# Causal masks and maxima in a routed attention kernel: who adds, who subtracts, who copies

## The chip, the cores and the metric

The program runs on one core of one Trainium2 chip. The metric is the device time of one execution in microseconds (us); a version is compared by the median of its runs. Engines are named as in the profile: PE (TensorE matmul, with PEld for its weight loads), DVE (VectorE), ACT (ScalarE), POOL (GpSimd), SP (SyncE, which here only issues transfers). PSUM is the memory that PE writes its results to, in banks of 512 fp32 columns; SBUF is the working memory.

## The reference

Sparse attention over 8 batches, 8 heads, 576 positions, 64 dimensions, then a mixture of experts over the 4608 tokens that it yields. Everything is fp32.

```python
scores = q @ k.T / 8
mask_local   = (rel >= 0) & (rel < 32)                              # heads 0-3, rel = row - column
mask_strided = (rel >= 0) & (column % 32 == row % 32)               # heads 4-7
scores = where(mask, scores, -1e9); scores -= max(scores)
x = softmax(scores) @ v                                             # (4608, 512)
do_compute = x @ w_skip > 0;  e = argmax(x @ w_gate)
out = x;  out[do_compute] += gate * relu(x @ w1[e]) @ w2[e]         # one of 8 experts per token
```

## The kernel before

**Units.** Attention is cut into 32 units, four to a batch (`UNITS`, line 33): local heads in blocks of 64 queries by 96 keys, blocks 0 to 3 (unit 0) and 4 to 8 (unit 1), and strided heads as 11 blocks of 54 by 54, blocks 0 to 5 (unit 2) and 6 to 10 (unit 3). A unit (b, u) is unit u of batch b. It passes through these functions:

- `qk` (line 186): on PE the scores of the unit (line 196, four 64x64 corners of the array in turn, fp32) into the PSUM tile S. S spans two banks and there is **one** of it. On DVE the mask is added on the way from S to the SBUF tile `sm` (lines 203, 205, 210: tables of 0 and -2^33), which frees S; then DVE takes the row maxima of `sm` (line 216), and POOL subtracts them in two halves (line 219), in place for local units, into the padded tile `frame` for strided ones.
- `tex` (line 224): PE transposes of the result into PSUM tiles T (line 239), ACT exponentials out of them (line 247).
- `pv` (line 252): PE matmuls with the values into the single PSUM tile PV (lines 269, 282), DVE divides by the row sums (lines 290 to 296) and frees PV.
- `xpose` (line 312): PE transposes (lines 327, 337) and ACT copies of the attention output; `score` (line 358): PE matmuls of a batch with the router weights (line 362), ACT copies (lines 366, 367).

**Routing.** `route1` turns the router scores of a group of batches (PE, line 382), copies them with ACT (line 384) and picks the expert on DVE in nine small instructions (lines 390 to 408), with a few small POOL ones (lines 413 to 417). `route2` counts ranks on PE (lines 426 to 433), gets slots on DVE (438 to 443) and POOL scatters the tokens into a table (line 456). `shift` (line 180) copies the values by 32 rows for odd blocks, in two ACT copies a batch (line 183). `wdma` fetches an eighth of an expert's weights into one of three buffers `raw`; `wsplit` (line 566) splits it into a high part (ACT, line 572) and a rest (DVE, line 573).

**Order.** A loop over the 32 units writes the program of PE, DVE and POOL in the order of the code (`manual_schedule`); ACT's order is chosen by a scheduler. Turn n does: `qk` of unit n+2 on PE; `tex` of unit n; `pv` of unit n-1; then, on DVE, the mask of unit n+2, the division of unit n-1, and the maxima of unit n+2; then `xpose` of unit n-2, the router scores of the last batch (turn of a unit 2), and the pieces of routing and of weight splitting that are due. I call "turn (b, u)" the turn whose `tex` is unit (b, u). Every engine works its own list strictly in order. After the loop the experts' matmuls (lines 631 to 633, 670, 674) run on PE until the end.

Of the kernel before, what the change touches and what calls it, by code (L numbers as in the profile page):

```python
# [23 lines left out]
HP = 64  # L24
LW = HP + ST
LB = S // HP
LV = 5
SQ = 3 * NA
SB = 11
SP = 6  # L30
UNITS = [(0, 0, 4), (0, 4, LB), (1, 0, 6), (1, 6, SB)]
# [8 lines left out]
COUNTED = {4: 3, 7: 5}  # L40
PB = 3
CB = 5
SPLITS = [(6, 0), (6, 1), (7, 0), (7, 2)]
FETCH = [(6, 0), (6, 1), (6, 3), (7, 0)]
CE = (96, 3)

# [51 lines left out]
def attn_moe(ctx: ExitStack, tc: tile.TileContext, q, k, vl, vh, vs, w9d, w1d, w2d, cst, out, NB=B):  # L98
    nc = tc.nc
    V, A, G, T = nc.vector, nc.scalar, nc.gpsimd, nc.tensor  # L100
# [9 lines left out]
    ident = con["id"]  # L110
    w9 = constp.tile([128, 4, 64], F32, name="w9")
    tri = constp.tile([128, 128], BF16, name="tri")
    oneb = constp.tile([128, 128], BF16, name="oneb")
    ebb = constp.tile([128, NE], BF16, name="ebb")
    runs = [constp.tile([128, NE], BF16, name=f"run{i}") for i in range(2)]
# [4 lines left out]
    def ps(tag, n=1):  # L120
        return psum.tile([128, n, 512] if n > 1 else [128, 512], F32, name=tag, tag=tag, bufs=bufs[tag])
# [14 lines left out]
        G.memset(fill[:, :, 1:2], 65536)  # L136
        return fill

    sms = [ap.tile([128, 2, (z - a) * (LW, SQ)[kind]], F32, name=f"sm{i}") for i, (kind, a, z) in enumerate(UNITS)]
    frame = [ap.tile([128, 2, 6, HP], F32, name=f"frame{i}") for i in range(2)]  # L140

    qt_, kt_, vt_ = {}, {}, {}
# [37 lines left out]
    def shift(b, k):  # L180
        r0, r1, d, c = SHIFTS[k]
        src, dst = vt_[b, 0][r0:r1, c:c + LV - 1], v2[b % 2][d:d + r1 - r0]
        A.copy(dst.rearrange("p u h c -> p (u h c)"), src.rearrange("p u h c -> p (u h c)"))


    def qk(b, pr):
        kind, b0, b1 = UNITS[pr]
        qt, kt = qt_[b, kind], kt_[b, kind]
        nq, win = ((HP, LW), (SQ, SQ))[kind]
        n = (b1 - b0) * win  # L190
        s = ps("S", 2)
        for blk in range(b0, b1):
            for j in range(2):
                for i in range(2):
                    p = slice(HP * i, HP * i + HP)
                    T.matmul(s[HP * (i ^ j):HP * (i ^ j) + HP, j, (blk - b0) * win:(blk - b0 + 1) * win],  # L196
                             lhsT=qt[p, j, blk * nq:blk * nq + HP], rhs=kt[p, j, blk * nq:blk * nq + win],
                             start=True, stop=True)
        yield
        sm = sms[pr]  # L200
        if kind == 0:
            if b0 == 0:
                V.tensor_tensor(sm, s[:, :, 0:n], con["ml"].unsqueeze(1).broadcast_to([128, 2, n]), op=ALU.add)
            else:
                V.tensor_tensor(sm.rearrange("p j (n w) -> p j n w", w=win),
                                s[:, :, 0:n].rearrange("p j (n w) -> p j n w", w=win),
                                con["ml"][:, LW:2 * LW].unsqueeze(1).unsqueeze(1).broadcast_to([128, 2, b1 - b0, LW]),
                                op=ALU.add)
        else:
            V.tensor_tensor(sm.rearrange("p j (n w) -> p j n w", w=win),  # L210
                            s[:, :, 0:n].rearrange("p j (n w) -> p j n w", w=win),
                            con["ms"].unsqueeze(1).unsqueeze(1).broadcast_to([128, 2, b1 - b0, win]), op=ALU.add)
        yield
        mx = ap.tile([128, 2, b1 - b0], F32, name="mx", tag="mx", bufs=4)
        sw = sm.rearrange("p j (n w) -> p j n w", w=win)
        V.tensor_reduce(mx, sw, axis=AX.X, op=ALU.max)
        e = sw if kind == 0 else frame[pr - 2][:, :, 0:b1 - b0, 0:win]
        for j in range(2):
            G.tensor_tensor(e[:, j], sw[:, j], mx[:, j].unsqueeze(2).broadcast_to([128, b1 - b0, win]), op=ALU.subtract)  # L219
        e_[b, pr] = e  # L220

    e_, pt_ = {}, {}
# [340 lines left out]
                tc.add_manual_dep(i, x.name, SYNC, reason="the tokens come first")  # L563
            raw_[key, j] = raw

    def wsplit(key, j0, j1):
        for j in range(j0, j1):
            raw = raw_.pop((key, j))
            pl, tg, nb = (early, "w1", 4) if j < 4 else (pool["h"], "w2", 2) if j < 6 else (pool["b"], "w2", 4)
            hi = pl.tile([128, 1024], F32R, name=tg + "h", tag=tg + "h", bufs=nb)  # L570
            lo = pl.tile([128, 1024], F32R, name=tg + "l", tag=tg + "l", bufs=nb)
            A.copy(hi, raw)  # L572
            V.tensor_tensor(lo, raw, hi.bitcast(F32), op=ALU.subtract)  # L573
            wt[key, j] = (hi, lo)

    def wload(key, e, j0, j1):
        for j in range(j0, j1):
# [207 lines left out]
    p = ps("T")  # L785
# [3 lines left out]
    def run(*gs):  # L789
        weave(gs, [])  # L790
# [17 lines left out]
    loadq(1, 0)  # L808
    loadk(1, 0)
    loadv(0, 1)  # L810
    for i in range(2):
        G.memset(frame[i], 0.0)
    V.memset(pvp, 0.0)
# [6 lines left out]
    for n, (b, pr) in enumerate(units):  # L820

        if pr % 2 == 0:
            if b + 1 < NB:
                loadv(b + 1, pr // 2)
            if n == 4:
                nc.sync.dma_start(table.rearrange("(p a n) c -> p a (n c)", p=128, a=5),
                                  fill.rearrange("p n c -> p (n c)").unsqueeze(1).broadcast_to(
                                      [128, 5, NE * ESTR // 160]))
        else:
            if n > 4:  # L830
                store(units[n - 4][0], units[n - 4][1] // 2)
# [12 lines left out]
        seq = [tex(b, pr)]  # L844
        if g and pr == 2:
            seq = [xpose(*units[n - 2])] + seq
        for x in front[:-1]:
            next(x)

        if len(front) > 1:  # L850
            run(seq.pop(0))
        next(front[-1])
        rank = []
        if ranked is not None:
            rank = [route2(ranked, of=COUNTED.get(b - 1))]
            for _ in range(tiles(ranked) + 1):
                next(rank[0])
            ranked = None

        if b > CB:  # L860
            run(*late)
            late = []
        for x in front:
            next(x, 0)
        run(*rank, *late, *front)
        late = []
        if b > 0 and pr == 2:
            seq = [score(b - 1, 0), score(b - 1, 1)] + seq
        if n > 1 and not (g and pr == 2):
            seq.append(xpose(*units[n - 2]))  # L870
        run(*seq)
        if g and pr == 2:
            late = [route1(g[0])]
            next(late[0])
        if g and pr == 3:
            if b > CB:
                run(route2(g[0], of=COUNTED.get(b)))
            else:
                ranked = g[0]
        if b == PB + 2 and pr == 0:  # L880
            pick(PB)
        if (b, pr) in SPLITS:
            j = SPLITS.index((b, pr))
            wsplit("e", j, j + 1)
        if b == CB + 2 and pr == 3:
            count(CB)
        if n == 0 or pr == 3 and b + 1 < NB:
            for m in range(2):
                shift(b + (n > 0), m)
        if n == 1:  # L890
            for g in range(len(GROUPS)):
# [12 lines left out]
        if b == CB + 2:  # L904
            if pr == 0:
                assert not sc_
            if pr == 1:
                rows("e", s0, *CE, eng=G)
                gather("e", "e", "e", last=(CB + 1) * S)
# [3 lines left out]
        scat(*sc_.pop(0))  # L913
    with tc.manual_schedule(engines={T.engine, A.engine, V.engine}):
        run(pv(*units[-1]), xpose(*units[-2]), xturn("e"), xpose(*units[-1]))
    store(NB - 1, 0)
    store(NB - 1, 1)
    wdma("e", e0, 5, 7, st_["e"]["taken"])
# [173 lines left out]
```

## Time and profile before

| | us |
|---|---|
| time, median of 3 runs | 452.54 (452.0 to 456.13) |
| the profiled execution: its own time | 450.83 |
| its span, first to last instruction | 449.1 |
| PE busy in the span | 414.5 (92%) |
| DVE / ACT / POOL busy | 257.5 / 203.7 / 162.9 |
| end of the attention loop on PE, about | 178 |
| waits of PE between 84 and 180 us, in the table of stretches | 17.1 |

How to read it: one execution, times from the start of its span. A group row gives a line, an engine, output<-input, the count, busy time, mean ns of one, and after the second bar the idle time just before with what ended it. A row of the timeline gives start, duration, engine, line, and in brackets the idle time before it. "PEclk" is the share of full clock that PE was granted. "issue" is idle time that the trace gives no cause for.

### The profile page before, as it was taken

How to read it: one execution, taken by the hardware profiler on the slowest of the kernel's cores; microseconds unless marked ns; L12 is line 12 of the kernel's file. 1: busy time of each engine (PE TensorE's matmuls, PEld its weight loads, DVE VectorE, ACT ScalarE, POOL GpSimd, SP SyncE). 2: the span in 40 equal slices, each digit the busy share in tenths (PEclk: the TensorE clock that was granted, in tenths of full speed). 3: DMA queues.
4: the chain of work that ended last, by engine and by line, in shares of the span. 5: the costliest groups of instructions: out<-in, count | busy, mean ns of one | idle time of the engine just before them, and what ended most of it. 6: DMA issues, size and time to landing. Idle time of an engine off the chain costs nothing.

```text
span 449.1 us, 12164 instructions
## 1 busy us (share of the span) xinstructions
PE 414.5 (92%) x4959; PEld 375.0 (83%) x4960; DVE 257.5 (57%) x522; ACT 203.7 (45%) x382; POOL 162.9 (36%) x205
## 2 busy tenths in 40 slices
PE   5979979998786877999999999999999999999994
PEld 3868868777665656889899799999999999999984
DVE  4576766658675675362476465464474564755611
ACT  1556555564544635451633343444444534544400
POOL 3443426563848485364023417014023023200201
PEclk8899998999996998899999999999999999999998
DMA  8999996988896323533558477446566466754201
GB/s 288 368 382 324 340 314 168 300 254 303 251 332 133 74 56 107 148 61 85 180 161 224 141 223 219 135 161 208 163 200 186 157 204 193 213 157 158 73 21 42
DMA packets 48600, 86.51 MB, mean 193 GB/s; under 512 B 9271, under 2 KB 25783, under 8 KB 48541
## 3 DMA queue, kind: packets, MB, share of 16 engines
q1 hardware_dynamic: 40861, 75.28, 53.1%
q0 software_dynamic: 7680, 10.42, 8.5%
q8 instruction: 40, 0.66, 0.6%
q14 instruction: 19, 0.16, 0.1%
HBM read 70.64 MB, written 15.63 MB: 192 GB/s over the span
## 4 chain that ended last, share of the span: by engine, by line
PE 69%; DMA 9%; DVE 6%; issue 6%; POOL 3%; SPq 3%; ACT 2%; POOLq 0%; DVEq 0%; ACTq 0%
PE S L631 15%; PE S L633 15%; PE S L632 15%; PE S L196 4%; PE T L239 4%; PE PV L269 3%; DMA out_dram<-x 3%; PE T L362 2%; DMA xg<-out_dram,tab 2%; PE T L625 2%; PE PV L723 2%; PE PV L282 2%; DVE x L296 1%; PE T L337 1%; POOL table L456 1%
## 5 line engine op out<-in xcount | busy, mean ns | idle before, releaser
L711 POOL DMA_INDIRECT out_dram<-ot,tab x25 | 28.0, 1121 | 152.5 <-DVE ot L709 136.5
L631 PE MATMUL S<-xh,w1h 128*128 128x342 f32 (+6 forms) x248 | 78.4, 316 | 0.2 <-DVE hl L644 0.2
L633 PE MATMUL S<-xh,w1l 128*128 128x342 f32 (+6 forms) x248 | 76.7, 309 | 0.0
L632 PE MATMUL S<-xl,w1h 128*128 128x342 f32 (+6 forms) x248 | 76.6, 309 | 0.0
L631 PE MATMUL S<-hh,w2h 128*128 128x288 f32 (+5 forms) x192 | 59.4, 310 | 0.0
L633 PE MATMUL S<-hh,w2l 128*128 128x288 f32 (+5 forms) x192 | 58.1, 303 | 0.0
L632 PE MATMUL S<-hl,w2h 128*128 128x288 f32 (+5 forms) x192 | 57.9, 302 | 0.0
L643 ACT ACTIVATE hh<-S 128x342 fp32r<-128x342 f32 (+6 forms) x64 | 27.9, 437 | 65.6 <-PE S L633 57.9
L573 DVE TENSOR_TENSOR w1l<-raw,w1h 128x1024 fp32r<-128x1024 f32 x32 | 39.0, 1224 | 22.2 <-ACT w1h L572 21.7
L631 PEld LDWEIGHTS S<-xh,w1h 128*128 128x128 f32 x248 | 46.9, 189 | 1.2 <-issue 0.6
L573 DVE TENSOR_TENSOR w2l<-raw,w2h 128x1024 fp32r<-128x1024 f32 x32 | 39.0, 1223 | 14.0 <-ACT w2h L572 9.2
L632 PEld LDWEIGHTS S<-xl,w1h 128*128 128x128 f32 x248 | 46.8, 189 | 0.1
L633 PEld LDWEIGHTS S<-xh,w1l 128*128 128x128 f32 x248 | 46.7, 188 | 0.0
L196 PE MATMUL S<-kt,qt 64*64 64x54 f32 (+1 forms) x1280 | 32.8, 245 | 13.4 <-DVE sm L210 8.2
L644 DVE SCALAR_TENSOR_TENSOR hl<-S,hh 128x342 fp32r<-128x342 f32 (+6 forms) x64 | 30.9, 484 | 24.1 <-ACT hh L643 22.7
L603 POOL DMA_INDIRECT xg<-out_dram,tab x25 | 31.9, 1275 | 33.2 <-issue 10.6
L456 POOL DMA_INDIRECT table<-pay,rdi x38 | 39.8, 1047 | 10.7 <-issue 8.3
L196 PEld LDWEIGHTS S<-kt,qt 64*64 64x64 f32 x1280 | 27.2, 143 | 19.1 <-DVE sm L210 9.3
L219 POOL TENSOR_TENSOR sm<-sm,mx 128x384 f32<-128x384 f32 (+1 forms) x32 | 28.4, 908 | 32.0 <-PE T L239 11.7
L633 PEld LDWEIGHTS S<-hh,w2l 128*128 128x128 f32 x192 | 36.2, 189 | 0.2 <-DVE w2l L573 0.2
L632 PEld LDWEIGHTS S<-hl,w2h 128*128 128x128 f32 x192 | 36.3, 189 | 0.0
L631 PEld LDWEIGHTS S<-hh,w2h 128*128 128x128 f32 x192 | 36.2, 188 | 0.1
(167 smaller groups left out, 845.9 us busy)
## 6 DMA issues: line engine op xcount, KB each, us to landing
raw<-in_w_dram SPq DMA_DIRECT2D x64, 512.0 KB
vt<-in_vs_dram SPq DMA_DIRECT2D x16, 390.0 KB
qt<-in_qp_dram SPq DMA_DIRECT2D x16, 304.0 KB
kt<-in_kp_dram SPq DMA_DIRECT2D x16, 297.0 KB
kt<-in_kp_dram SPq DMA_DIRECT2D x14, 304.0 KB
vt<-in_vl_dram SPq DMA_DIRECT2D x16, 260.0 KB
out_dram<-x SPq DMA_DIRECT2D x8, 512.0 KB
qt<-in_qp_dram SPq DMA_DIRECT2D x14, 288.0 KB
```

Of the source, the lines that this page charges most:

```text
L196: T.matmul(s[HP * (i ^ j):HP * (i ^ j) + HP, j, (blk - b0) * win:(blk - b0 + 1) * win], lhsT=qt[p, j, blk * nq:blk * nq + HP], rhs=kt[p, j ...
L219: G.tensor_tensor(e[:, j], sw[:, j], mx[:, j].unsqueeze(2).broadcast_to([128, b1 - b0, win]), op=ALU.subtract)
L239: T.transpose(t[:w, x * 128:(x + 1) * 128], a, ident)
L456: i = G.indirect_dma_start(out=table, out_offset=bass.IndirectOffsetOnAxis(ap=di[:, t:t + 1], axis=0), in_=pay[:, t, :], in_offset=None, b ...
L573: V.tensor_tensor(lo, raw, hi.bitcast(F32), op=ALU.subtract)
L603: i = G.indirect_dma_start(out=xg[:s["P"], t, :], out_offset=None, in_=out[0:last, :], in_offset=bass.IndirectOffsetOnAxis(ap=s["tab"][:s[ ...
L631: T.matmul(p, lhsT=a[0], rhs=b[0], start=start, stop=False)
L632: T.matmul(p, lhsT=a[0], rhs=b[1], start=False, stop=False)
L633: T.matmul(p, lhsT=a[1], rhs=b[0], start=False, stop=stop)
L643: A.activation(s["hh"][:, f, :C], p[:, :C], AF.Relu)
L644: V.scalar_tensor_tensor(s["hl"][:, f, :C], p[:, :C], 0.0, s["hh"][:, f, :C].bitcast(F32), op0=ALU.max, op1=ALU.subtract)
L711: i = G.indirect_dma_start(out=out, in_=ot[:P], in_offset=None, bounds_check=NTOK - 1, oob_is_err=False, out_offset=bass.IndirectOffsetOnA ...
```

## The change

- PE writes the mask into S first, from bf16 copies of the tables (`mlb`, `msb`) times a bf16 identity (`idb`), four matmuls a unit, and the scores accumulate onto it. The copies are made by DVE at the start.
- DVE takes the maxima straight from S and then subtracts them straight from S; POOL's subtraction is gone, and so are the additions. S is free after the subtraction.
- The value copies of `shift` move from ACT to POOL.
- PE's turning of the router scores moves from the end of one turn to the next turn, behind its `tex`.
- `wsplit` inside the loop is cut in two: ACT's part stays in turns (6, 0), (6, 1), (7, 0), DVE's part comes a turn later, and the fourth piece (turn (7, 2) before) is done after the loop.

```diff
-SPLITS = [(6, 0), (6, 1), (7, 0), (7, 2)]
+CASTS = [(6, 0), (6, 1), (7, 0)]
+RESTS = [(6, 1), (6, 2), (7, 1)]
...
+    mlb = constp.tile([128, 4 * LW], BF16, name="mlb")
+    msb = constp.tile([128, SQ], BF16, name="msb")
+    idb = constp.tile([128, HP], BF16, name="idb")
...
-        A.copy(dst.rearrange("p u h c -> p (u h c)"), src.rearrange("p u h c -> p (u h c)"))
+        G.tensor_copy(dst.rearrange("p u h c -> p (u h c)"), src.rearrange("p u h c -> p (u h c)"))
...
         s = ps("S", 2)
+        hide = mlb if b0 == kind == 0 else (mlb[:, LW:2 * LW], msb)[kind].unsqueeze(1).broadcast_to([128, b1 - b0, win])
+        for j in range(2):
+            for i in range(2):
+                p, g = slice(HP * i, HP * i + HP), slice(HP * (i ^ j), HP * (i ^ j) + HP)
+                T.matmul(s[g, j, 0:n], lhsT=idb[p], rhs=hide[p], start=True, stop=False)
         for blk in range(b0, b1):
...
-                             start=True, stop=True)
-        yield
-        sm = sms[pr]
-        if kind == 0:
-            if b0 == 0:
-                V.tensor_tensor(sm, s[:, :, 0:n], con["ml"].unsqueeze(1).broadcast_to([128, 2, n]), op=ALU.add)
...
+                             start=False, stop=blk == b1 - 1)
         yield
         mx = ap.tile([128, 2, b1 - b0], F32, name="mx", tag="mx", bufs=4)
-        sw = sm.rearrange("p j (n w) -> p j n w", w=win)
+        sw = s[:, :, 0:n].rearrange("p j (n w) -> p j n w", w=win)
         V.tensor_reduce(mx, sw, axis=AX.X, op=ALU.max)
-        e = sw if kind == 0 else frame[pr - 2][:, :, 0:b1 - b0, 0:win]
-        for j in range(2):
-            G.tensor_tensor(e[:, j], sw[:, j], mx[:, j].unsqueeze(2).broadcast_to([128, b1 - b0, win]), op=ALU.subtract)
+        e = sms[pr].rearrange("p j (n w) -> p j n w", w=win) if kind == 0 else frame[pr - 2][:, :, 0:b1 - b0, 0:win]
+        V.tensor_tensor(e, sw, mx.unsqueeze(3).broadcast_to([128, 2, b1 - b0, win]), op=ALU.subtract)
...
+    V.tensor_copy(mlb, con["ml"])
+    for i in range(2):
+        V.tensor_copy(idb[HP * i:HP * i + HP], ident[HP * i:HP * i + HP, HP * i:HP * i + HP])
+    V.tensor_copy(msb, con["ms"])
...
         if len(front) > 1:
             run(seq.pop(0))
+        if late:
+            next(late[0])
         next(front[-1])
...
             late = [route1(g[0])]
-            next(late[0])
...
-        if (b, pr) in SPLITS:
-            j = SPLITS.index((b, pr))
-            wsplit("e", j, j + 1)
+        if (b, pr) in RESTS:
+            j = RESTS.index((b, pr))
+            wrest("e", j, j + 1)
+        if (b, pr) in CASTS:
+            j = CASTS.index((b, pr))
+            wcast("e", j, j + 1)
...
         run(pv(*units[-1]), xpose(*units[-2]), xturn("e"), xpose(*units[-1]))
+        wsplit("e", 3, 4)
```

`wcast` is ACT's line of `wsplit`, `wrest` DVE's.

Three places show how the lists move. The first is DVE's list in turn (0, 2) and at the start of turn (0, 3) (`sm_80`, `sm_81`: the two local units of batch 1; `x`: output of the division). Before:

```order
L203 TENSOR_TENSOR sm_80<-S,cs 128x768
L290 TENSOR_SCALAR rc<-PV 128x12
L291 RECIPROCAL rc<-rc 128x12
L296 TENSOR_TENSOR x_293<-PV,rc 128x3x128 x2
L216 TENSOR_REDUCE mx<-sm_80 128x8
L205 TENSOR_TENSOR sm_81<-S,cs 128x960
```

With the change (line 211 takes the maxima, 213 subtracts, 284 to 290 divide):

```order
L211 TENSOR_REDUCE mx<-S 128x8
L213 TENSOR_TENSOR sm_83<-S,mx 128x768
L284 TENSOR_SCALAR rc<-PV 128x12
L285 RECIPROCAL rc<-rc 128x12
L290 TENSOR_TENSOR x_308<-PV,rc 128x3x128 x2
L211 TENSOR_REDUCE mx<-S 128x10
L213 TENSOR_TENSOR sm_84<-S,mx 128x960
```

Two passes over S now stand between the scores and the next use of S, where one stood; the division comes behind both.

The second is DVE's list across turns (6, 0) and (6, 1), at the first split of expert weights (`w1l`). Before:

```order
L216 TENSOR_REDUCE mx<-sm_82 128x12
L573 TENSOR_TENSOR w1l<-raw,w1h 128x1024
L210 TENSOR_TENSOR sm_83<-S,cs 128x540
L290 TENSOR_SCALAR rc<-PV 128x2x4
L291 RECIPROCAL rc<-rc 128x2x4
L296 TENSOR_TENSOR x_2574<-PV,rc 128x2x128 x2
```

With the change:

```order
L211 TENSOR_REDUCE mx<-S 128x10
L213 TENSOR_TENSOR frame_86<-S,mx 128x2x5x54
L284 TENSOR_SCALAR rc<-PV 128x2x4
L285 RECIPROCAL rc<-rc 128x2x4
L290 TENSOR_TENSOR x_2636<-PV,rc 128x2x128 x2
L572 TENSOR_TENSOR w1l<-raw,w1h 128x1024
L211 TENSOR_REDUCE mx<-S 128x8
```

The subtraction for the weights stood ahead of a step that frees S, and stands now behind one, a turn later.

The third is turn (6, 3), where batch 6 is routed. DVE's list before (lines 405 to 408 are the end of `route1`, 205 adds the mask of unit (7, 1)):

```order
L405 TENSOR_TENSOR rohb<-cs,rmw 128x40
L407 TENSOR_REDUCE rrs<-rohb 128x8
L408 TENSOR_TENSOR run_69<-run_70,rrs 128x8
L205 TENSOR_TENSOR sm_81<-S,cs 128x960
L290 TENSOR_SCALAR rc<-PV 128x12
L291 RECIPROCAL rc<-rc 128x12
```

With the change:

```order
L399 TENSOR_TENSOR rohb<-cs,rmw 128x40
L401 TENSOR_REDUCE rrs<-rohb 128x8
L402 TENSOR_TENSOR run_72<-run_73,rrs 128x8
L211 TENSOR_REDUCE mx<-S 128x10
L213 TENSOR_TENSOR sm_84<-S,mx 128x960
L284 TENSOR_SCALAR rc<-PV 128x12
```

PE's list there before (382 turns the router scores, 196 makes the scores of unit (7, 1), 239 is `tex` of unit (6, 3), 282 `pv`):

```order
L382 MATMUL T<-cs,s_89 128x41 x5
L196 MATMUL S<-kt_2290,qt_2287 64x96 x20
L239 MATMUL T<-cs,frame_85 118x128 x4
L239 MATMUL T<-cs,frame_85 54x128 x2
L282 MATMUL PV<-vt_2185,pts 64x65 x24
```

With the change (four mask matmuls, line 200, stand ahead of the first row):

```order
L205 MATMUL S<-kt_2337,qt_2334 64x96 x20
L233 MATMUL T<-cs,frame_86 118x128 x4
L233 MATMUL T<-cs,frame_86 54x128 x2
L376 MATMUL T<-cs,s_90 128x41 x5
L276 MATMUL PV<-vt_2238,pts 64x65 x24
```

`route1` of batch 6 still stands ahead of the work on S on DVE, and its input (line 376) is now turned behind `tex`, not ahead of the turn's scores. In the groups before batch 6 `route1` stands behind the work on S and the division, with the change as before.

More of the change, by code (lines that the diff above doesn't have):

```diff
@@ L137, in setup @@
         return fill
-    sms = [ap.tile([128, 2, (z - a) * (LW, SQ)[kind]], F32, name=f"sm{i}") for i, (kind, a, z) in enumerate(UNITS)]
+    sms = [ap.tile([128, 2, (z - a) * LW], F32, name=f"sm{i}") for i, (kind, a, z) in enumerate(UNITS[0:2])]
     frame = [ap.tile([128, 2, 6, HP], F32, name=f"frame{i}") for i in range(2)]
@@ L197, in qk @@
                              lhsT=qt[p, j, blk * nq:blk * nq + HP], rhs=kt[p, j, blk * nq:blk * nq + win],
-                             start=True, stop=True)
-        yield
-        sm = sms[pr]
-        if kind == 0:
-            if b0 == 0:
[L203 to L212, printed above, removed]
+                             start=False, stop=blk == b1 - 1)
         yield
         mx = ap.tile([128, 2, b1 - b0], F32, name="mx", tag="mx", bufs=4)
-        sw = sm.rearrange("p j (n w) -> p j n w", w=win)
+        sw = s[:, :, 0:n].rearrange("p j (n w) -> p j n w", w=win)
         V.tensor_reduce(mx, sw, axis=AX.X, op=ALU.max)
-        e = sw if kind == 0 else frame[pr - 2][:, :, 0:b1 - b0, 0:win]
-        for j in range(2):
-            G.tensor_tensor(e[:, j], sw[:, j], mx[:, j].unsqueeze(2).broadcast_to([128, b1 - b0, win]), op=ALU.subtract)
+        e = sms[pr].rearrange("p j (n w) -> p j n w", w=win) if kind == 0 else frame[pr - 2][:, :, 0:b1 - b0, 0:win]
+        V.tensor_tensor(e, sw, mx.unsqueeze(3).broadcast_to([128, 2, b1 - b0, win]), op=ALU.subtract)
         e_[b, pr] = e
@@ L564, in wdma, with wcast @@
             raw_[key, j] = raw
-    def wsplit(key, j0, j1):
+    def wcast(key, j0, j1):
         for j in range(j0, j1):
-            raw = raw_.pop((key, j))
+            raw = raw_[key, j]
             pl, tg, nb = (early, "w1", 4) if j < 4 else (pool["h"], "w2", 2) if j < 6 else (pool["b"], "w2", 4)
@@ L572, in wsplit, with wrest @@
             A.copy(hi, raw)
-            V.tensor_tensor(lo, raw, hi.bitcast(F32), op=ALU.subtract)
             wt[key, j] = (hi, lo)
+    def wrest(key, j0, j1):
+        for j in range(j0, j1):
+            hi, lo = wt[key, j]
+            V.tensor_tensor(lo, raw_.pop((key, j)), hi.bitcast(F32), op=ALU.subtract)
+    def wsplit(key, j0, j1):
+        for j in range(j0, j1):
+            wcast(key, j, j + 1)
+            wrest(key, j, j + 1)
     def wload(key, e, j0, j1):
```

## The prediction

> **What bounds the kernel now.** First the page's line of busy times: PE leads, and no other engine is near it.
>
> ```profile
> PE 414.5 (92%) x4959; PEld 375.0 (83%) x4960; DVE 257.5 (57%) x522; ACT 203.7 (45%) x382; POOL 162.9 (36%) x205
> ```
>
> An average says little about a stage, so next the table of stretches (after the length: busy time of PE, PEld, DVE, ACT, POOL; then granted clock, DMA share, GB/s). The change touches the attention loop alone, which ends at about 178 us.
>
> ```profile
> 36.00:48.00 12.00, 12.00 (x291) 9.88 (x282) 8.53 (x16) 6.89 (x15) 4.01 (x6) 1.00 0.96 327
> 132.00:144.00 12.00, 7.91 (x147) 6.61 (x141) 7.73 (x17) 6.12 (x9) 10.20 (x12) 0.76 0.64 184
> ```
>
> From 36 to 48 us PE has no idle time at all: there each PE instruction added costs its full length, and relief of DVE or POOL is worth nothing. From 132 to 144 us a third of PE's time is idle, at a clock of 0.76: only there can unloading others pay. PE's single waits, from the timeline (start, length, row, then the idle time before it):
>
> ```profile
> 109.02 0.89 PE L196 MATMUL S<-kt,qt 64*64 64x54 f32 x40 [0.93 <-DVE sm L210]
> 114.82 0.99 PE L196 MATMUL S<-kt,qt 64*64 64x96 f32 x32 [1.49 <-DVE sm L210]
> 131.71 0.80 PE L196 MATMUL S<-kt,qt 64*64 64x54 f32 x40 [1.18 <-DVE sm L210]
> 139.82 1.65 PE L196 MATMUL S<-kt,qt 64*64 64x96 f32 x32 [3.80 <-DVE sm L210]
> 149.78 0.50 PE L382 MATMUL T<-cs,s 41*128 41x41 f32 x5 [1.50 <-ACT s L367]
> 158.37 0.80 PE L196 MATMUL S<-kt,qt 64*64 64x54 f32 x40 [0.75 <-DVE sm L210]
> ```
>
> Five times PE waits for S to be freed by DVE, 8.2 us together, and here once for ACT. Most of its other waits in the loop are marked "issue" and have no cause in the trace; I leave them as they are.
>
> **The change, term by term.** The sum starts from the profiled execution, 450.83 us.
>
> *A: masks on PE.* Four bf16 matmuls a unit, of 384, 480, 324 and 270 columns in the four units: 1458 columns a batch in each corner of the array. No bf16 matmul of this shape is in the trace. Rows for the price (score matmuls from the chain of waits, two records each; and two successive experts' matmuls):
>
> ```profile
> 38.79 2.00 PE T L362 x16
> 41.38 0.99 PE S L196 x40
> 188.21 0.29 PE L633 MATMUL S<-xh,w1l 128*128 128x288 f32 x1
> 188.34 0.30 PE L631 MATMUL S<-xh,w1h 128*128 128x288 f32 x1
> ```
>
> The experts' matmuls start 0.13 us apart for 288 columns, 0.457 ns a column; the program declares their operands as a reduced type, and I take bf16 at the same pace. If the four corners run wholly side by side, a batch pays 1458 x 0.457 = 0.67 us, the loop 5.3 us; one after another, 21.3 us. The fp32 rows decide between: line 362 makes eight matmuls of 288 columns in 2.00 us, two halves of the array at a time, so one alone is 0.25 to 0.5 us, 1.9 to 3.8 of the fast ones; line 196 makes four corners of 96 columns in 0.99 / 5 = 0.198 us, 4.5 fast ones, where four in turn would be 7.6 to 15.2. Corners thus share 1.7 to 3.4-fold. I take 3.4: 5.3 x 4 / 3.4 = 6.3 us, 28/32 of it after the first four units: **+5.5** (4.6 to 11).
>
> *B: the start.* The chain of waits from the first scores on:
>
> ```profile
> 5.99 0.97 DVE sm L203
> 7.96 1.33 PE S L196 x40
> 10.52 0.46 PE S L196 x4
> 18.39 0.82 PE S L196 x32
> ```
>
> ```profile
> 11.57 0.22 DVE L131 CAST tri<-cs 128x128 bf16<-128x128 f32 x1
> ```
>
> Today unit (0, 0)'s scores are ready before the tables arrive, just ahead of DVE's first addition at 5.99, and S is freed by one addition. With the change PE must first wait for DVE's bf16 copies of the tables and the identity: three casts, 0.7 us by the row of a small one. Masks and scores take 1.6 (1.33 x 32/40 for the scores, 0.5 for the masks, an estimate: A at half its pace, as the clock is low here), and S goes round by scores, maxima, subtraction: 6.7 + 1.6 + 0.96 + 0.95 = 10.2 for the second unit's scores (7.96 now), + 1.8 + 1.15 + 1.16 = 14.4 for the third's (10.52); `tex` and the fourth unit follow likewise, until unit (1, 0)'s scores come at about 21.9, not 18.39. **+3.5** (2.5 to 4.5). This is loss without cover.
>
> *DVE in the steady loop: nothing.* The addition goes, a subtraction of the same shape comes. Prices for the largest unit:
>
> ```profile
> L205 DVE TENSOR_TENSOR sm<-S,cs 128x960 f32<-128x960 f32 x6 | 6.9, 1157 | 13.3 <-PE S L196 8.4 <-PE T L239 4.9
> L216 DVE TENSOR_REDUCE mx<-sm 128x10 f32<-128x960 f32 x6 | 6.9, 1144 | 0.0
> ```
>
> What changes is how long S is held: 1.2 us now, with the change maxima plus subtraction, 1.14 + 1.16 + 0.14 of handover = 2.44 us for the largest unit. What covers it is PE's work until it wants S again, here in such a turn (first and last of four rows: from `tex` to the next scores):
>
> ```profile
> 42.37 0.80 PE T L239 x6
> 44.93 0.85 PE S L196 x48
> ```
>
> 44.93 - 42.37 = 2.56 us. It fits by 0.12 us; the other three units are smaller, and PE's work in their turns is longer. The maxima from PSUM I price as those from SBUF: addition and maximum of the same shape differ by under 2% though one reads PSUM.
>
> *C: the weight split in turn (6, 0).* DVE stands still for ACT and then subtracts, ahead of the step that frees S:
>
> ```profile
> 136.93 0.95 ACT w1h L572
> 137.91 1.23 DVE w1l L573
> 142.52 2.69 PE PV L269 x39
> 53.93 1.48 PE PV L269 x39
> ```
>
> DVE's part a turn later finds ACT's done: the wait of 3.80 goes. With it goes the low clock behind it: the same 39 records of line 269 took 2.69 us here and 1.48 at 53.93, line 196 took 1.65, the same 32 records 0.99 at 114.82: 1.9 us in these two lines. Clock in stretches after idle times of 3.80, 1.84 and 2.19 us:
>
> ```profile
> 140.00:146.00 6.00, 6.00 (x84) 5.37 (x85) 4.05 (x9) 1.08 (x2) 4.87 (x5) 0.57 0.76 148
> 66.00:70.00 4.00, 4.00 (x64) 3.44 (x65) 2.71 (x8) 1.19 (x2) 2.41 (x4) 0.58 0.58 223
> 30.00:32.00 2.00, 1.55 (x38) 1.31 (x41) 0.75 (x5) 0.24 (x1) 0.00 (x0) 1.00 1.08 384
> ```
>
> So a long wait costs twice, though not each one does. **-5.7** (-3.8 if the clock doesn't come back).
>
> *D: router scores turned later.* PE's wait for ACT's copies ahead of line 382 goes, as ACT gets PE's next scores and `tex` for cover (about 2 us, against 1.50 at most):
>
> ```profile
> PE T L382 <- ACT s L367: 2.9, 3, 1.5
> PE T L382 <- ACT s L367: 0.5, 1, 0.5
> ```
>
> (total, times, longest; after and before 84 us.) **-3.4.**
>
> *E: turn (6, 3).* Here `route1` stands on DVE ahead of the work on S.
>
> ```profile
> 150.21 1.06 PE L196 MATMUL S<-kt,qt 64*64 64x96 f32 x40
> 150.74 0.21 DVE L390 TENSOR_TENSOR s<-T,s 128x45 f32<-128x45 f32 x1 [3.06 <-ACT s L384]
> 152.73 1.16 DVE L205 TENSOR_TENSOR sm<-S,cs 128x960 f32<-128x960 f32 x1
> 154.03 0.92 PE L196 MATMUL S<-kt,qt 64*64 64x54 f32 x48
> ```
>
> Now: scores at 150.21, `route1` from 150.74 to 152.73, addition, S free, next scores at 154.03: 3.8 us. With the change `route1`'s input comes 1.3 (mask, scores) + 0.8 (`tex`) + 0.5 (turning) + 0.4 (ACT) = 3.0 us after that start, then 2.0 for `route1`, 2.44 for S: next scores at 7.45, where PE's own work ends at 5.0. A new wait of 2.45 us; queued behind it is all of PE's next turn. It swallows the 0.75 at 158.37; I add 1.0, half of C's clock loss. **+2.7** (0.5 to 4.5).
>
> [...]
>
> *F: S and POOL in the routing turns.* `route1` of the earlier groups stands behind the work on S. At 109 and 131 us DVE did maximum and addition behind `route1`, then S was free; now maximum and subtraction: about the same (-0.5 by the order). PE's waits of 0.23 to 0.30 us at line 239 for POOL's subtraction end: 0.75. **-1.2** (-4 to +3).
>
> *G: value copies on POOL.*
>
> ```profile
> L183 ACT COPY v<-vt 64x1040 f32<-64x1040 f32 (+1 forms) x16 | 16.9, 1058 | 1.4 <-DMA vt<-in_vl_dram 1.1
> L219 POOL TENSOR_TENSOR sm<-sm,mx 128x384 f32<-128x384 f32 (+1 forms) x32 | 28.4, 908 | 32.0 <-PE T L239 11.7 <-DVE mx L216 9.8 <-PE PV L282 3.5
> 0.88 1.41 POOL L812 MEMSET frame<- 128x768 f32 x2 [0.29 <-POOLq L1078]
> ```
>
> POOL's price lies between its memset (0.70 us for 768, so 0.95 for 1040) and its subtraction (0.91 for 432 on average, 2.2 for 1040); nearest is the one-stream memset. Two copies, 2 us, up to 4.4, begin when the turn before a batch ends, and `pv` of that batch's first unit comes a whole turn later (over 4 us). **0** (to +3 where `route1` holds POOL). ACT loses 16.9 us that PE hardly waited for. POOL loses its subtractions, 28.4 us for the local units and the strided ones' besides; its scatters and gathers come earlier, but none stands among PE's waits above.
>
> Sum: 5.5 + 3.5 - 5.7 - 3.4 + 2.7 - 1.2 + 0 = +1.4, 452.2 us for an execution like the profiled one. That one lies 1.7 below the median of the runs, so the forecast of a median is **453.9**. Its own range, from the terms' ends: 449.5 to 458.5.
>
> **Rivals.** *S is held too long* (slower). The margin of 0.12 us in term "DVE" is thin. If the two passes over S are 20% dearer when both read PSUM, 2.9 us, seven batches lose 0.35 each (2.4), and five routing or picking turns, where DVE is late anyway, lose the further pass, 0.7 each (3.5): +5.8 on the sum, median 459.7. It decides from a hold of 2.56 us on. For it: one S tile, and 8.2 us of waits for it today. Against: those waits stood behind routing or weights, never behind an addition alone. [...]
>
> *Masks don't share the array* (slower): A is 21.3 x 28/32 = 18.6, median 467.0. Against it line 196.
>
> *Most waits go* (faster): A at 4.6, B at 2.5, no new wait in turn (6, 3) (E = -0.75), the waits at 109, 114 and 131 us gone wholly (F = -3.6 - 0.75): 4.6 + 2.5 - 5.7 - 3.4 - 0.75 - 4.35 = -7.1, median 445.4. For it: POOL's subtractions no longer run beside DVE, where an instruction on eight numbers took 0.80 us while one of them ran, and this on the way to the wait at 114.82.
>
> ```profile
> 112.12 0.80 DVE L488 TENSOR_SCALAR first<-key,pmx 1x8 f32<-1x8 f32 x1
> 112.16 1.42 POOL L219 TENSOR_TENSOR frame<-sm,mx 128x324 f32<-128x324 f32 x2 [1.85 <-DVE pmx L487]
> ```
>
> Against it: with the change DVE does more ahead of each release of S, not less.
>
> **Chances.** Forecast 0.45; S held too long 0.25, unshared masks 0.04; most waits gone 0.26. A measurement of this kernel tells about 1% (4.5 us) from no change, so faster 0.26, same 0.45, slower 0.29. The range 445.5 to 460 covers the forecast's own range and the middle of both near rivals.
>
> **What would show it.** Line 200's busy time near 6 us (A); unit (1, 0)'s scores near 22 us (B); no wait for S at the former 139.8 us and full clock behind it (C); none at the turning of router scores (D); a wait of over 2 us for S once, after batch 6's routing (E); no PE wait for S in turns without routing. I am wrong if PE waits for S in ordinary turns, if line 200 costs over 10 us, or if the loop ends before 172 us.

## The result, and the profile after

The changed kernel took **479.72 us** (median of 4 runs, 477.24 to 489.15), the kernel before, beside it, 454.34: ratio **1.054** (95% interval 1.043 to 1.064). Forecast were 453.9, and 460 as the upper end. The ratio leaves out executions that the chip ran in a slower state, here the one of 489.15. The profiled execution took 477.24 us, its span is 475.5. Since the kernel before took 446.5 to 454.6 us from one set of runs to the next, versions are compared by their ratio to the kernel before in the same set.

The page after, line of busy times:

```profile
PE 432.7 (91%) x5087; PEld 388.3 (82%) x5088; DVE 260.9 (55%) x526; ACT 187.6 (39%) x366; POOL 129.9 (27%) x157
```

PE is busy 18.2 us longer, with 128 matmuls more; POOL lost 33 us. The two stretches that the prediction began with:

```profile
36.00:48.00 12.00, 12.00 (x251) 9.80 (x249) 7.89 (x14) 6.43 (x14) 0.00 (x0) 1.00 0.88 285
132.00:144.00 12.00, 11.12 (x218) 9.21 (x218) 7.19 (x14) 5.10 (x12) 0.00 (x0) 0.86 0.89 249
```

The first is full as before. The second lies, with the loop longer, in another part of the work. So I go by units instead: the four stretches in which the loop lost its time, the first three from one unit's masks to the next one's ((4, 0), (6, 0), (7, 0)), the last from those of (7, 3) on:

```profile
76.10:89.61 13.51, 9.72 (x104) 7.33 (x104) 4.18 (x9) 3.03 (x8) 7.71 (x9) 0.75 0.73 188
126.49:138.67 12.18, 8.81 (x102) 6.83 (x102) 4.32 (x10) 2.27 (x6) 4.23 (x5) 0.86 0.82 217
151.29:168.97 17.68, 12.84 (x103) 8.54 (x102) 6.40 (x12) 3.85 (x7) 5.84 (x6) 0.71 0.20 56
181.72:192.90 11.18, 7.66 (x92) 5.92 (x91) 3.97 (x13) 2.91 (x7) 5.04 (x6) 0.69 0.23 56
```

About a hundred matmul records stand in each, as many as in 4.4 to 5.0 us at the pace of the first table (x251 in 12 us). The third from close by, the timeline of PE (first, middle and last rows), POOL, DVE and ACT:

```profile
151.48 0.43 PE L205 MATMUL S<-kt,qt 64*64 64x96 f32 x5
152.28 0.39 PE L205 MATMUL S<-kt,qt 64*64 64x96 f32 x4 [0.36 <-issue]
...
154.48 0.36 PE L205 MATMUL S<-kt,qt 64*64 64x96 f32 x3 [1.06 <-issue]
...
160.21 0.63 PE L205 MATMUL S<-kt,qt 64*64 64x96 f32 x6 [0.41 <-issue]
```

```profile
148.71 1.08 POOL L450 DMA_INDIRECT table<-pay,rdi  x1 [0.16 <-POOL v L187]
150.10 0.98 POOL L450 DMA_INDIRECT table<-pay,rdi  x1 [0.30 <-issue]
...
157.79 0.97 POOL L450 DMA_INDIRECT table<-pay,rdi  x1 [0.30 <-issue]
```

```profile
157.37 0.17 DVE L284 TENSOR_SCALAR rc<-PV 128x8 f32<-128x8 f32 x1 [6.69 <-remote]
160.19 0.67 ACT L333 COPY xT<-T 128x432 f32<-128x432 f32 x2 [9.88 <-remote]
```

Thirty-two score matmuls, 0.83 us at (2, 0), take from 151.48 to 160.84, in handfuls of 1 to 6, 0.7 or 1.4 us from one to the next; the idle time between them is marked "issue", so the profile names no semaphore for it. ("remote" in the rows of DVE and ACT marks a wait that an event ended which the profile could put down to no instruction.) Meanwhile POOL issues eight scatters 1.28 us apart, with nothing between. DVE and ACT begin 6.7 and 8.8 us after the PE instruction whose result they need. The same pattern stands in the other three stretches, where the rows marked "remote" begin 4.1 to 6.4 us after it. POOL had subtractions between its scatters before; the change took them away.

### The profile page after: what moved, and what is told of

The parts are those of the page before. It is cut to its first block, busy times and chain, and to the rows that moved or that the text cites. A ratio compares the mean times of both kernels' runs of the same rounds, so it can differ in the third digit from the quotient of the medians.

```text
span 475.5 us, 12302 instructions
## 1 busy us (share of the span) xinstructions
PE 432.7 (91%) x5087; PEld 388.3 (82%) x5088; DVE 260.9 (55%) x526; ACT 187.6 (39%) x366; POOL 129.9 (27%) x157
## 4 chain that ended last, share of the span: by engine, by line
PE 80%; issue 7%; DVE 6%; DMA 3%; ACT 2%; POOL 1%; SPq 1%; POOLq 0%; ACTq 0%; DVEq 0%
PE S L634 15%; PE S L636 15%; PE S L635 15%; PE S L205 6%; PE T L233 6%; PE PV L263 6%; PE T L356 3%; PE T L331 2%; DMA out_dram<-x 2%; PE PV L276 2%; PE S L200 2%; PE T L628 2%; PE PV L726 2%; PE T L321 2%; DVE mx L211 1%
## 5 line engine op out<-in xcount | busy, mean ns | idle before, releaser
L211 DVE TENSOR_REDUCE mx<-S 128x8 f32<-128x768 f32 (+3 forms) x32 | 29.1, 910 | 40.3 <-PE S L205 21.2
L205 PE MATMUL S<-kt,qt 64*64 64x54 f32 (+1 forms) x1280 | 38.8, 249 | 8.6 <-issue 8.4
L205 PEld LDWEIGHTS S<-kt,qt 64*64 64x64 f32 x1280 | 33.5, 150 | 13.0 <-issue 12.3
L606 POOL DMA_INDIRECT xg<-out_dram,tab x25 | 33.5, 1341 | 36.8 <-PE S L636 10.6
L647 DVE SCALAR_TENSOR_TENSOR hl<-S,hh 128x342 fp32r<-128x342 f32 (+6 forms) x64 | 30.9, 483 | 20.4 <-ACT hh L646 19.1
```

Of the source, the lines that this page charges most:

```text
L606: i = G.indirect_dma_start(out=xg[:s["P"], t, :], out_offset=None, in_=out[0:last, :], in_offset=bass.IndirectOffsetOnAxis(ap=s["tab"][:s[ ...
L647: V.scalar_tensor_tensor(s["hl"][:, f, :C], p[:, :C], 0.0, s["hh"][:, f, :C].bitcast(F32), op0=ALU.max, op1=ALU.subtract)
```

## The experiments

**1. A wait each turn (paced).** The theory from here on, "scatters in a row": scatters that POOL issues back to back hold up the other engines.

```diff
+        if sc_ and n + LA < len(units):
+            G.tensor_copy(pace, mx_[units[n + LA]][0:1, 0, 0:1])
         for _ in range(3 if b > CB else 2):
```

> The changed kernel, with one tiny GpSimd copy a turn (one number of that turn's maxima) ahead of the turn's scatters, so that GpSimd can issue at most two (in the last batches three) of them before it waits for the turn's scores. Theory 'scatters in a row': in the changed kernel GpSimd, freed of its subtractions, issues 5 to 8 scatters back to back, and during each such row PE, DVE and ACT almost stop; four rows cost some 25 us. Then this kernel takes 446 to 460 us and PE has no cluster of idle times marked 'issue' beside scatters. Rival 'value copies': GpSimd's copies of 2.15 us are what holds the loop; they stay, so 475 to 484. Rival 'masks and S' (mask matmuls and the longer hold of S cost it): 475 to 484 too.

Measured 1.039 (1.029 to 1.048), 471.0 us: neither. POOL's rows say why: the maxima were there before POOL asked, so the copy rarely waited and the row stayed a row, with 1.33 us from scatter to scatter across the copy:

```profile
77.62 1.00 POOL L452 DMA_INDIRECT table<-pay,rdi  x1 [0.30 <-issue]
78.62 0.17 POOL L907 COPY pace<-mx 1x1 f32<-1x1 f32 x1
78.95 0.98 POOL L452 DMA_INDIRECT table<-pay,rdi  x1 [0.16 <-issue]
80.24 0.97 POOL L452 DMA_INDIRECT table<-pay,rdi  x1 [0.30 <-issue]
```

The run didn't test what it was made for; it shows that a wait is no pause.

**2. Pauses behind pairs (filler).**

```diff
-        for _ in range(3 if b > CB else 2):
+        for m in range(3 if b > CB else 2):
             if sc_ and n + 1 < len(units):
                 scat(*sc_.pop(0))
+                if m:
+                    for _ in range(3):
+                        G.memset(junk, 0.0)
```

> The changed kernel, with three GpSimd memsets of 768 elements (0.70 us each) behind each scatter that isn't the first of its turn: GpSimd waits for nothing new, but two scatters are followed by 2.1 us of other work. Theory 'scatters in a row': a pause between pairs is enough, 448 to 462. Rival 'it is the place in the turn that matters, not the pause': no better than the changed kernel, 474 to 484.

Measured 1.012 (1.003 to 1.021), 458.5 us, as the theory had it: more work on POOL, the same scatters, and by the ratios four fifths of the loss gone.

**3. Two parts of the change alone (moves).** Terms C and D in the kernel before, with `wcast` and `wrest` as in the change:

```diff
-SPLITS = [(6, 0), (6, 1), (7, 0), (7, 2)]
+CASTS = [(6, 0), (6, 1), (7, 0)]
+RESTS = [(6, 1), (6, 2), (7, 1)]
...
+        if late:
+            next(late[0])
         next(front[-1])
...
             late = [route1(g[0])]
-            next(late[0])
```

> The kernel before, with two parts of the change alone: the weight split in two halves a turn apart (term C) and the router scores' turning moved later (term D). Masks, subtractions on GpSimd and value copies on ACT stay as before, so GpSimd's subtractions still stand between its scatters. Theory 'scatters in a row': no loss, and terms C and D as predicted (-9.1): 441 to 449. Rival 'the moves themselves cost': 460 or more. Rival 'the moves' gains are hidden': 451 to 457.

Measured **0.988** (0.983 to 0.994), 448.6 us: 1.2% under the kernel before, and far under the changed one.

**4. Whose instructions don't come (probe).**

```diff
+        if pr == 2 and b in (3, 5, 6):
+            for _ in range(14):
+                V.memset(probe[0], 0.0)
+                A.copy(probe[2], probe[1])
         front = [qk(*units[n + LA])] if n + LA < len(units) else []
```

> The changed kernel with 14 memsets on DVE and 14 copies on ACT (256 elements each, of tiles that nothing else uses) at the start of turns (3, 2), (5, 2) and (6, 2), where in the changed kernel the rows of scatters begin; they wait for no other engine. One look, its time isn't compared. Two accounts of why DVE and ACT start up to 9 us late in a row of scatters: if their own instructions don't arrive, these 28 too come with gaps of 0.3 us and more between them; if only the news of PE's finished work arrives late, they follow each other at the pace of their own lengths, and the gap comes behind them, at the first instruction that waits for PE.

The 14 memsets fell into the first row of scatters, where PE came in single matmuls (PE's rows, first and last):

```profile
77.46 5.36 DVE L852 MEMSET probe<- 128x256 f32 x14
...
80.05 0.22 PE L263 MATMUL PV<-v,ptl 96*64 96x65 f32 x1 [0.43 <-issue]
...
83.00 0.26 PE L263 MATMUL PV<-vt,ptl 96*64 96x65 f32 x1 [1.12 <-issue]
...
84.51 0.96 DVE L211 TENSOR_REDUCE mx<-S 128x8 f32<-128x768 f32 x1 [1.69 <-remote]
```

Fourteen in 5.36 us, 0.38 us each, without a gap; then DVE waits for scores that PE had finished at 78.0. So these instructions of DVE's own came, and the news from PE did not. Whether a longer list would have come too, the run doesn't show. ACT's copies were put elsewhere by its scheduler and say nothing.

**5. Scatters that write nothing (nowrite).**

```diff
-        G.tensor_scalar(mk, mw, 0.0, 65536.0, op0=ALU.is_equal, op1=ALU.mult)
+        G.tensor_scalar(mk, mw, 0.0, 65536.0, op0=ALU.is_ge, op1=ALU.mult)
```

> The changed kernel with every scatter's slot number out of bounds (the comparison that marks dropped tokens is true for all), so that the scatters are issued as before and write nothing: it leaves out the filling of the table, and the experts work on the table's initial rows. If the rows of scatters cost PE through the issuing on GpSimd, the idle times marked 'issue' stay: 470 to 484. If they cost it through the writes that they start, these go: 448 to 462.

Measured 0.990 (0.985 to 0.995), 441.3 us beside 446.6, the account of the writes (it also spares the experts some transfers). POOL issues the same row, and PE is busy throughout:

```profile
80.95 0.97 POOL L450 DMA_INDIRECT table<-pay,rdi  x1 [0.30 <-issue]
82.23 0.97 POOL L450 DMA_INDIRECT table<-pay,rdi  x1 [0.30 <-issue]
```

```profile
78.00:84.00 6.00, 6.00 (x122) 4.78 (x114) 3.67 (x8) 3.10 (x8) 4.48 (x6) 1.00 0.64 166
```

In the changed kernel the same six microseconds, beside the same row, hold 27 matmul records and 2.80 us of PE:

```profile
78.00:84.00 6.00, 2.80 (x27) 1.92 (x27) 0.00 (x0) 0.00 (x0) 3.90 (x4) 0.81 0.83 185
```

So it is not the issuing on GpSimd: it takes scatters that really write.

**6. Half the rows (half_rows).**

```diff
+        G.memset(mk[64:128], 65536.0)
```

> The changed kernel with the slot numbers of half of each scatter's 128 rows out of bounds (a memset of 64 partitions of the drop mark): as many scatters, 1.28 us apart in the same rows of 5 to 8, and half the rows written. It leaves out half of the table's entries, so half of the tokens get no expert's output. If the stall counts rows written (128 rows each 1.9 us went without a stall, 67 rows a us; here 64 each 1.28 us, 50 a us), it goes: 0.98 to 1.005 of the kernel before, and PE idles nowhere beside scatters. If it counts scatters that write at all, it stays: 1.04 to 1.06.

Measured 0.985 (0.979 to 0.991), 440.7 us beside 446.5. Six scatters 1.28 us apart, and no stall:

```profile
81.92 0.97 POOL L451 DMA_INDIRECT table<-pay,rdi  x1 [0.30 <-issue]
83.20 0.97 POOL L451 DMA_INDIRECT table<-pay,rdi  x1 [0.30 <-issue]
```

```profile
82.00:88.00 6.00, 6.00 (x124) 4.52 (x120) 3.62 (x6) 3.53 (x7) 2.83 (x3) 1.00 0.92 215
```

So not every scatter that writes costs PE the same. But the counts in the expectation are slots, not rows: a token that gets no expert is out of bounds in every kernel. By the sizes of the packets in the trace (16 a scatter, from 32 bytes without a row to 128 with eight), the 38 scatters of the changed kernel write 2381 rows, 63 each on average; of these, 1263 stand in the half of the slots that is written here. And rows written per time do not decide. In the changed kernel the five scatters from 179.31 us on write 187 rows, 29 a us, and PE idles beside them; the first six of the next experiment write 445, 39 a us, and it does not.

```profile
186.53 0.78 PE L205 MATMUL S<-kt,qt 64*64 64x54 f32 x16 [0.94 <-issue]
```

The packet sizes of the changed kernel add up if each packet takes its eight slots from one half of the 128; then half of each scatter's packets carry no row at all here, which may be what counts. No run tells that apart.

**7. Even spacing (fill1).**

```diff
                 scat(*sc_.pop(0))
+                G.memset(junk, 0.0)
```

> The changed kernel with one GpSimd memset (768 elements) behind each scatter, so about 2.1 us from scatter to scatter, where the pairs with three memsets had 1.3 and 3.5 (4.8 a pair) and the changed kernel 1.28 throughout. Account 'backlog' (each scatter leaves work that is done at some fixed pace, and PE stalls while two or more lie waiting): 2.1 us is nearly the same mean pace as the pairs' 2.4, so 455 to 464. Account 'any scatter behind another costs PE the same': 38 scatters as before, 472 to 482.

Measured 1.010 (1.005 to 1.016), 451.5 us beside 446.6: by the ratio in the range of "backlog". Whole scatters 1.9 us apart, six in a row, leave no idle time marked "issue" on PE while they are issued. What is left is another wait, for the value copy (term G), which POOL, behind the scatters, began, by the profile, only when these had landed:

```profile
95.20 2.15 POOL L187 COPY v<-vt 64x1040 f32<-64x1040 f32 x2 [6.53 <-DMA table<-pay,rdi]
```

```profile
97.41 0.27 PE L263 MATMUL PV<-v,ptl 96*64 96x65 f32 x1 [3.06 <-POOL v L187]
```

**8. The masks twice (double)**, in the kernel of experiment 2: a second set of four mask matmuls with zero weights:

```diff
+                T.matmul(s[g, j, 0:n], lhsT=zerob[p], rhs=hide[p], start=False, stop=False)
```

> The kernel with memsets behind pairs of scatters, and four more mask matmuls a unit that add zeros (bf16, weights zero, same columns): term A once more. If the four corners share the array as forecast, 5 to 7 us over the kernel without them, 463 to 467; if they share it wholly, 4.5 to 5.5; if one after another, 18 to 22. The longer scores also put off DVE's start on S, a part of the hold: nothing where PE waits for nobody.

Measured 1.033 (1.027 to 1.038), against 1.012 (1.003 to 1.021) for the kernel without them in another set: 2.1%, some 9 us, with intervals that allow 3 to 16. Too loose to price term A. Its rows do: from one set to the next PE advances 0.19 us, and from there to the scores 0.16.

```profile
38.76 0.36 PE L201 MATMUL S<-mlb,idb 64*64 64x384 bf16 x4
38.95 0.33 PE L205 MATMUL S<-mlb,zerob 64*64 64x384 bf16 x4
39.11 0.83 PE L210 MATMUL S<-kt,qt 64*64 64x96 f32 x32
```

**9. Value copies back on ACT (copies_act)**, in the kernel of experiment 2:

```diff
-        G.tensor_copy(dst.rearrange("p u h c -> p (u h c)"), src.rearrange("p u h c -> p (u h c)"))
+        A.copy(dst.rearrange("p u h c -> p (u h c)"), src.rearrange("p u h c -> p (u h c)"))
```

> The kernel with memsets behind pairs of scatters, and the value copies back on ACT (term G undone, nothing else). Forecast G = 0: within 2 us of the kernel without this, 456 to 460. Rival 'GpSimd's copies of 2.15 us cost the loop something': 452 to 455. Rival 'they relieve ACT': 461 to 465.

Measured 1.004 (1.000 to 1.007), under the 1.012 of experiment 2 in another set: it points to a cost of the copies on POOL of some 4 us, though the two intervals overlap.

**10. Both (spaced):** the memset of experiment 7 and the copies on ACT.

> The changed kernel with one GpSimd memset of 768 elements behind each scatter (1.9 us from scatter to scatter) and the value copies back on ACT. Account so far: scatters 1.9 us apart cost PE nothing visible, and with the copies on ACT no weight of a batch waits behind them on GpSimd (a wait of 3.06 us). Then 0.985 to 1.000 of the kernel before. Rival 'even spacing is no better than pairs with pauses': 1.004, as the pairs with copies on ACT had.

**11. And two mends (best):** masks of the first three units added by DVE as before (`old`), and in batch 6 the work on S ahead of `route1`:

```diff
+        old = b == 0 and pr < 3
...
-        if b > CB:
-            run(*late)
-            late = []
         for x in front:
```

> The spaced kernel, and two mends: units (0, 0) to (0, 2) get their masks from DVE's addition as in the kernel before, so that PE doesn't start on DVE's bf16 copies (term B), and in batch 6 route1 stands behind the work on S on DVE, not ahead of it (term E). Forecast: B gives 3 us back, E 2 us: 0.975 to 0.990 of the kernel before, 4 to 6 us under the spaced kernel. Rival 'the late routing puts the gathers off by as much': within 2 us of the spaced kernel.

Measured 1.000 (0.997 to 1.004) for the spaced one, at the upper end of what was expected; beside fill1's 1.010 (1.005 to 1.016) it agrees with some 4.5 us for the copies on POOL, though the two ratios are of different sets. The best one took **0.988** (0.981 to 0.995), 446.1 us, 4.0 under the spaced one. But it is no better than experiment 3, which has no masks on TensorE at all. Putting the work on S first only moved the wait of batch 6, from S to the routing:

```profile
150.97 0.19 PE L432 MATMUL T<-rohb,tri 128*128 128x40 bf16 x1 [2.31 <-DVE rohb L411]
```

**12. Pauses where POOL subtracts (moves_spaced):** experiment 3 with three memsets of 256 elements behind each scatter:

```diff
                 scat(*sc_.pop(0))
+                for _ in range(3):
+                    G.memset(fill, 0)
```

> The kernel before with terms C and D alone, and 0.9 us of GpSimd memsets behind each scatter: masks and subtractions stay on DVE and GpSimd. Some 4 us of PE's idle time beside pairs and threes of scatters should go, against 0.988 without the memsets: 0.976 to 0.986. If memsets on GpSimd put its subtractions off instead, 0.988 or more. It also tells what the masks on TensorE are worth when nothing else is in the way: if the best kernel of this row is faster, they are worth something.

Measured 1.023 (1.012 to 1.033): the second account. In the list of waits, 60 to 180 us (total, times, longest):

```profile
PE T L240 <- POOL sm L220: 8.5, 9, 3.0
```

The subtractions came late. The pauses did what they were for: in the same stretch PE's idle time marked "issue" fell from 8.0 us in experiment 3 to 1.5. But with the subtractions on POOL most of the pauses are there already, and more of them cost more than they bring.

**13. The kernel before, with rows (before_row):**

```diff
-        for _ in range(3 if b > CB else 2):
+        for _ in range(9):
```

> The kernel before, with one number changed: up to nine scatters a turn, not two or three, so that GpSimd issues a group's scatters in one row of 5 to 9. Theory 'scatters in a row': PE's idle times marked 'issue' appear here too, and the loop gets 10 to 25 us longer, 1.02 to 1.06. Rival 'only the changed kernel suffers from them': no such idle times, only waits for GpSimd's late subtractions, 1.00 to 1.02.

Measured 1.038 (1.029 to 1.046), 466.7 us, and the same trickle without any of the change. From 60 to 200 us PE's waits for POOL's subtraction of local units stay at 0.9 us (0.7 before), so it is not that these came late:

```profile
124.18 0.22 PE L269 MATMUL PV<-v,ptl 96*64 96x65 f32 x1 [1.09 <-issue]
125.61 0.27 PE L269 MATMUL PV<-v,ptl 96*64 96x65 f32 x1 [1.08 <-issue]
127.04 0.27 PE L269 MATMUL PV<-v,ptl 96*64 96x65 f32 x1 [0.94 <-issue]
```

## Why the prediction was wrong, point by point

**The step that failed is in term G:** "POOL loses its subtractions [...]; its scatters and gathers come earlier, but none stands among PE's waits above." I asked what waits *for* a scatter, and not what a scatter does to others when several follow at once. The price, worked out from stretches of the changed kernel and of half_rows, whose scatters stall nothing: masks of (4, 0) to (4, 1) 13.5 us against 5.8, of (6, 0) to (6, 1) 12.2 against 5.9, of (7, 0) to (7, 1) 17.7 against 6.7, and from the masks of (7, 3) to the first expert matmul 26.3 against 19.3. That is 32 of the 33.2 us by which that matmul starts later than in half_rows. Against the whole kernels, 1.054 to 0.985 is 31 us, of which a part is work that half_rows leaves out; against fill1, with the same work, 1.054 to 1.010 is 20 us, and fill1 pays for its memsets. The term was put at 0 to +3, with no room for this. The range was too narrow by its own terms as well: their ends add up to 447 to 471, not 449.5 to 458.5. The measured time lies beyond these too.

**The trace of before showed it.** I had written of the idle times marked "issue" that they "have no cause in the trace; I leave them as they are". Here they are beside a row of three, at 158.59, 159.96 and 161.25, with "remote" waits of DVE and ACT:

```profile
161.25 1.09 POOL L456 DMA_INDIRECT table<-pay,rdi  x1 [0.30 <-issue]
...
161.41 0.26 PE L269 MATMUL PV<-v,ptl 96*64 96x65 f32 x1 [0.40 <-issue]
162.13 0.22 PE L269 MATMUL PV<-v,ptl 96*64 96x65 f32 x1 [0.37 <-issue]
...
163.07 1.35 ACT L247 ACTIVATE ptl<-T 96x512 f32<-96x512 f32 x3 [4.82 <-remote]
```

POOL subtracts from 162.36 on, and within a microsecond DVE and ACT go on. None of the three rivals held either: the slower ones had S or the masks for a cause.

**A, masks on PE: +5.5 forecast, right.** From masks to scores PE advances 0.19, 0.23, 0.16 and 0.14 us in the four units (38.75 to 38.94 for the first), 0.72 a batch, 5.0 in seven. The forecast's 0.67 a batch for corners wholly side by side is nearly met, so they share better than the 3.4-fold taken. "Line 200's busy time near 6" was a bad test: it is 12.2, since busy time counts the overlapping ends (the row at 38.75 is 0.36 us long, and the scores begin 0.19 after its start).

**B, the start: +3.5 forecast, 4.6 measured**, just above its range. Unit (1, 0)'s scores start at 22.88, before at 18.32. In half_rows, with the same start, they come at 21.91, so an execution can differ by a microsecond. The waits, as the chain had them (casts, then S twice):

```profile
6.52 0.75 PE L200 MATMUL S<-mlb,idb 64*64 64x384 bf16 x4 [1.78 <-DVE idb L816]
10.62 0.61 PE L200 MATMUL S<-mlb,idb 64*64 64x480 bf16 x4 [2.07 <-DVE sm L213]
15.31 0.49 PE L200 MATMUL S<-msb,idb 64*64 64x324 bf16 x4 [2.48 <-DVE sm L213]
```

**DVE steady, 0: right where no scatters are in the way.** Outside the start and the routing turns PE waits for S once, behind a row of scatters that had let DVE begin late; half_rows has no wait there. The thin cover of 0.12 us held.

```profile
96.19 0.49 PE L200 MATMUL S<-msb,idb 64*64 64x324 bf16 x4 [0.78 <-DVE sm L213]
```

**C, D and E together: -6.4 forecast; -5.3 measured** in moves (0.988; from -7.8 to -2.9). It has C and D whole, and E in part: `route1` comes late there too, but S is held for one pass, not two. The wait of 3.80 us in the weight turn is gone; from the scores of (6, 0) to those of (7, 0) moves needs 20.4 us, before 25.0. In the changed kernel the turning of the router scores is down to 0.2 us of idle time:

```profile
L376 PE MATMUL T<-cs,s 41*128 41x41 f32 x38 | 3.5, 235 | 0.2
```

E's new wait came where it was forecast, 2.45 us by the working, 2.38 by the trace:

```profile
176.46 0.33 PE L200 MATMUL S<-msb,idb 64*64 64x324 bf16 x4 [2.38 <-DVE sm L213]
```

The full clock that C was to bring back did not show in the changed kernel, as the row of scatters fell there (0.71 from 151.29 on).

**F, -1.2: not settled apart.** Of the waits for S ahead of the scores of (5, 3), (6, 0) and (6, 3), 0.93, 1.49 and 1.18 us, the first is gone, in place of the second stands idle time beside a row of scatters, and the third is 0.68; one of 0.70 is new ahead of (3, 3). PE waits for POOL's subtraction no more. No run undid this alone.

**The copies of G, 0 (to +3): mis-sized, about +4** where scatters are spaced (experiments 7, 9 and 10, by ratios from different sets): the copies stand behind the scatters in POOL's list.

With the scatters spaced the sum is nearly right: 0.3% forecast (453.9 over 452.54), 1.0% measured in fill1. That is in part luck, as fill1 also has memsets on POOL that the sum does not know. The masks on TensorE show no gain here either way: best and moves both stand at 0.988, with intervals of about 0.7% to either side.

## What to carry to other kernels

Work that you take from an engine may have been the pause between its transfers: when an engine gets free, list what it will then issue back to back, and look in the trace of before for what happens where two or three such already meet. Idle time that the profile gives no cause for is a question to ask before the change is costed; lay it beside the other queues' rows. Take a change apart before judging it: its moves of weight split and routing were worth 1.2%, while the part that gave it its name showed no gain.

## What was not expected of the hardware

Beside scatters that pile up, TensorE does a quarter to a fifth of its matmuls in the same time, and DVE and ACT begin 4.1 to 8.8 us after the results that they need: 27 matmul records in 6 us beside a row of scatters, where nowrite has 122 and half_rows 124 beside theirs. It takes scatters that write, close together. Whole ones 1.28 us apart stall PE (2.80 us busy of those 6.00); whole ones 1.9 us apart (six in fill1, with no idle time marked "issue" while they are issued) or half-empty ones 1.28 us apart (6.00 busy of 6.00) hardly do; as many that write nothing do not (6.00 of 6.00). Rows of 16 bytes per time are not the measure (29 a us with a stall, 39 without, experiment 6), and the load of the transfer engines is not either: in the third stretch of the result they were busy for 20% and moved 56 GB/s. The limit is not sharp. Late in a row of nine scatters 1.9 us apart (experiment 10) a little of it is there:

```profile
87.24 0.33 PE L276 MATMUL PV<-vt,pts 54*64 54x65 f32 x4 [0.26 <-issue]
87.98 0.27 PE L276 MATMUL PV<-vt,pts 54*64 54x65 f32 x2 [0.41 <-issue]
```

Nor does every row show it: in the kernel before, five scatters 1.3 us apart between 178.0 and 184.5 us, beside transposes and 0.3 us expert matmuls, left PE busy for 6.36 of 6.50 us. Perhaps longer matmuls hide it; no run tests that.

```profile
178.00:184.50 6.50, 6.36 (x38) 6.07 (x38) 3.44 (x14) 3.03 (x8) 5.04 (x5) 0.64 0.33 73
```

By which path the rows reach TensorE stays open, and no run here changed the size of the writes. That PE's instructions come late is a guess: it would explain the trickle, but not why in experiment 4 a DVE whose own memsets ran on began only at 84.51 on scores that PE had finished at 78.0.
